# A windowed-attention backward kernel: stores moved to SyncE's queue a step later, gradient loads held behind a transpose

## The chip, the cores and the metric

The kernel runs on one core of one Trainium2 chip. The core has five engines with their own instruction queues: TensorE (PE in the profile, with PEld for its weight loads), VectorE (DVE), ScalarE (ACT), GpSimd (POOL) and SyncE (SP, which only issues transfers and waits). Transfers between device memory and on-chip memory are carried by 16 DMA engines; SP and ACT issue onto hardware queues (q1 is SP's, q10 is ACT's), GpSimd onto a software queue (q0). An instruction queue is in order: while an instruction waits for a semaphore or is being issued, everything behind it on that engine waits too.

The metric is device time in microseconds (us) of one execution, lower is better. Before the change three executions took 1948.42, 1941.60 and 1948.11 us, median 1948.11.

## The reference, cut to what matters

`x` and `grad_out` are 256 x 256 x 384 images in bf16. Both are cut into 1024 windows of 8 x 8 tokens. Each window does single-head attention over its 64 tokens with 384 channels, and the outputs are the forward result and the gradients for `x`, `wqkv` and `wo`:

```python
xw  = windows of x                      # (1024, 64, 384)
qkv = xw @ wqkv;  q, k, v = split(qkv)
p   = softmax(q @ k.T * C ** -0.5)      # (1024, 64, 64)
out = (p @ v) @ wo, windows put back    # out_0
out_1, out_2, out_3 = vjp(out)(grad_out)  # d x, d wqkv, d wo
```

## The kernel before, in words

**Tiling.** Windows are taken eight at a time, as a *quad*: four tiles of 128 partitions, each holding two windows of 64 tokens. There are 128 quads. `load` (L122) brings a quad's `x` into `xq` with four DMAs of 96 KB on SP's queue and its `grad_out` into `dq` with four on GpSimd's queue. One such DMA covers 16 image rows of 8 tokens of 384 channels, that is 128 rows of 768 bytes. `xq` has ten buffers, `dq` six.

**Algebra.** The projections are folded into 384 x 384 weight products (`A_sb`, `AT_sb`, `B_sb`, `BT_sb`) at the start. Per quad the kernel needs `x` and `grad_out` with channels on the partitions (`xT`, `dT`), which `load_turn` (L129) makes with two DMA transposes on SP's queue; for the first quads (`G_ON_PE`, `X_ON_PE`) TensorE does it. `dT` has two buffers, `xT` three.

**Stages.** The work is software-pipelined over quads in `step(c, b, a, ahead)` (L334), called for i = -1 to 128 with a = quad i+1, b = quad i, c = quad i-1, ahead = quad i+3:

- `scores`, `soft` and `uv` of quad i (b); at the end of the softmax `turn` (L237) transposes `ps` into `PS` by a DMA transpose on SP.
- `project(0)` of quad i+1 (a), which reads `dT`; later `project(1)`, which reads `xT`; `gather` on VectorE packs both into `zy`, and `to_tokens` (L169) transposes `zy` into `tok` by the largest DMA transpose, on SP.
- `load(ahead)`: the eight loads of quad i+3.
- `attend` of quad i-1 (c), in two halves, tiles (0, 1) and (2, 3): all products that need `PS` and `tok`. Its results leave PSUM by ScalarE and VectorE copies into `o` and `d` buffers of the pool `ob`, which has eight of each; a quad uses four of each. Each half then issues its stores on GpSimd's queue (L298 to L305): four in the first half, five in the second, seven of them 96 KB and two of 48 KB.
- `filler` (L326) runs pieces of the weight gradients (`gf_group`) between.

**Order.** The schedule is manual: each engine executes its instructions in the order in which the program emits them. So SP's order in every step of the middle is `PS` of quad i, four `x` loads of quad i+3, `tok` of quad i+1, then (from `load_turn` at the top of the next step) `dT` and `xT` of quad i+3: eight DMAs per step. GpSimd's order is four `dq` loads, four stores, five stores. Every DMA of a queue is given one of eight completion semaphores in rotation and waits until the DMA that had it before has landed.

Of the kernel before, what the change touches and what calls it, by code (L numbers as in the profile page):

```python
# [11 lines left out]
BF16 = mybir.dt.bfloat16  # L12
# [10 lines left out]
def kernel(  # L23
# [21 lines left out]
    nc = tc.nc  # L45
# [9 lines left out]
    sm = ctx.enter_context(tc.tile_pool(name="sm", bufs=2))  # L55
# [18 lines left out]
    def fetch_weights():  # L74
        nc.sync.dma_start(out=w_sb[:, :, columns(2)], in_=w_in[:, :, columns(2)])
        nc.scalar.dma_start(out=wo_sb[:], in_=wo.rearrange("(m p) n -> p m n", p=P))
        for k in (0, 1):
            nc.scalar.dma_start(out=w_sb[:, :, columns(k)], in_=w_in[:, :, columns(k)])
# [32 lines left out]
    def weight_rest():  # L111
        weight_product(B_sb, wT[2], wo_sb, None)
        weight_product(AT_sb, wT[1], wT[0], scale)

    def windows(ap, st, first, count=2):
        row, col = st["at"]
        return ap[0, row + WIN * first:row + WIN * (first + count), col:col + WIN, :]

    LO, HI = slice(0, WT), slice(WT, P)
    OTHER = {0: HI, WT: LO}  # L120

    def load(st):  # L122
        st["xq"] = xq = grp.tile([P, QUAD, C], BF16, tag="xq", name="xq", bufs=2 * GQ + 4)
        st["dq"] = dq = qp.tile([P, QUAD, C], BF16, tag="dq", name="dq", bufs=6)
        for t in range(QUAD):
            nc.sync.dma_start(out=xq[:, t, :], in_=windows(x, st, 2 * t))
            nc.gpsimd.dma_start(out=dq[:, t, :], in_=windows(grad_out, st, 2 * t))  # L127
# [55 lines left out]
    def over_k(ap, n=P):  # L183
        return ap.unsqueeze(2).broadcast_to([n, QUAD, WT])

    def soft(st, step):
        sd = st["sd"]
        if step == 0:
# [53 lines left out]
    def operand(st, n, t, h):  # L242
        if n in ("PT", "ST"):
            return st["PS"][h, t, int((n == "ST") == (h == LO)), :]
        if n in ("z", "y"):
            return st["tok"][h, int(n == "y"), :, t, :]
        return st[n][h, t, :]

    def attend(st, pair):
        if pair[0] == 0:  # L250
            st["Uq"] = grp.tile([P, QUAD, C], BF16, tag="Uq", name="Uq")
            st["Wq"] = grp.tile([P, QUAD, C], BF16, tag="Wq", name="Wq")

        def bank(name):
            return ring.tile([P, C], F32, tag="r", name=name)

        def slot(straight, crossed, start=False, stop=False):
            for h in (LO, HI):
                dst, lhs, rhs, t = straight
                products = [(h, dst[h, :], lhs, rhs, t, {"start": True, "stop": True})]  # L260
                lhs, rhs, t = crossed
                o = OTHER[h.start]
                dst = pd[int((t == t0) == (h == LO))]
                products.append((o, dst[o, :], lhs, rhs, t, {"start": start, "stop": stop}))
                for o, dst, lhs, rhs, t, flags in products if h == LO else products[::-1]:
                    nc.tensor.matmul(dst, lhsT=operand(st, lhs, t, h), rhs=operand(st, rhs, t, h), **flags)  # L266

        def keep(name, src):
            sb = ob.tile([P, C], BF16, tag=name, name=name)
            nc.scalar.copy(out=sb[:], in_=src[:])  # L270
            return sb

        t0, t1 = pair
        pw = {t: bank("pw") for t in pair}
        pu = {t0: bank("pu")}
        pd = [bank("pd") for outer in (0, 1)]
        po = {t0: bank("po")}
        pu[t1] = bank("pu")
        po[t1] = bank("po")
        slot((pw[t0], "Pb", "dq", t0), ("Pb", "z", t0), start=True)  # L280
        nc.scalar.copy(out=st["Wq"][:, t0, :], in_=pw[t0][:])  # L281
        slot((pw[t1], "Pb", "dq", t1), ("dS", "y", t0))
        nc.vector.tensor_copy(out=st["Wq"][:, t1, :], in_=pw[t1][:])
        slot((pu[t0], "ST", "xq", t0), ("Pb", "z", t1), start=True)
        nc.vector.tensor_copy(out=st["Uq"][:, t0, :], in_=pu[t0][:])
        slot((po[t0], "PT", "uq", t0), ("dS", "y", t1))
        o0 = keep("o", po[t0])
        slot((pu[t1], "ST", "xq", t1), ("ST", "vq", t0), stop=True)
        nc.vector.tensor_copy(out=st["Uq"][:, t1, :], in_=pu[t1][:])
        slot((po[t1], "PT", "uq", t1), ("ST", "vq", t1), stop=True)  # L290
        o1 = keep("o", po[t1])
        inner = keep("d", pd[0])
        if t0 == 0:
            st["mid"], st["rim"] = [ob.tile([P, C], BF16, tag="d", name="d") for k in range(2)]
        upper, lower = (st["rim"], st["mid"]) if t0 == 0 else (st["mid"], st["rim"])
        nc.scalar.copy(out=lower[LO, :], in_=pd[1][LO, :])
        (nc.scalar.copy if t0 else nc.vector.tensor_copy)(out=upper[HI, :], in_=pd[1][HI, :])
        nc.gpsimd.dma_start(out=windows(out_0, st, 2 * t0), in_=o0[:])  # L298
        nc.gpsimd.dma_start(out=windows(out_0, st, 2 * t1), in_=o1[:])
        nc.gpsimd.dma_start(out=windows(out_1, st, 2 * t0 + 1), in_=inner[:])  # L300
        if t0 == 0:
            nc.gpsimd.dma_start(out=windows(out_1, st, 0, 1), in_=st["rim"][HI, :])
        else:
            nc.gpsimd.dma_start(out=windows(out_1, st, 3), in_=st["mid"][:])
            nc.gpsimd.dma_start(out=windows(out_1, st, 7, 1), in_=st["rim"][LO, :])  # L305

    fill = []

# [17 lines left out]
    def filler(n):  # L326
        while n and fill:
            try:
                next(fill[0])
                n -= 1  # L330
            except StopIteration:
                fill.pop(0)

    def step(c, b, a, ahead):  # L334


        def on(st):
            return (lambda f, *r: f(st, *r)) if st is not None else (lambda f, *r: None)
        C_, B, A = on(c), on(b), on(a)
        B(scores)  # L340
        B(soft, 0)
        if b is not None and c is None:
            weight_rest()
        B(uv, 0, 0)
        B(uv, 0, 1)
        B(soft, 1)
        B(uv, 1, 0)
        B(uv, 1, 1)
        B(soft, 2)
        B(soft, 3)  # L350
        B(uv, 2, 0)
        B(uv, 2, 1)
        B(uv, 3, 0)
        B(uv, 3, 1)
        B(soft, 4)
        for mo in range(CK):
            A(project, 0, mo)
        B(soft, 5)
        B(turn)
        if ahead is not None:  # L360
            load(ahead)
        filler(1)
        C_(attend, (0, 1))
        A(gather, 0)
        for mo in range(CK):
            A(project, 1, mo)
        A(gather, 1)
        A(to_tokens)
        filler(1)
        C_(attend, (2, 3))  # L370

    G_ON_PE, X_ON_PE = 4, 1
    EV = {"z": "AAA", "y": "AAA", "u": "AAAA", "v": "AAAA", "o": "AAAA", "U": "DDDD", "W": "DDDD", "d": "AAAA"}
    quads = [(row, col) for row in range(0, H, 2 * WIN * QUAD) for col in range(0, W, WIN)]
    sts = [{"at": q, "i": i} for i, q in enumerate(quads)]
    n = len(sts)
    AHEAD = 3
# [40 lines left out]
    with tc.manual_schedule(engines=MANUAL):  # L418
        fetch_weights()
        warm_up(9)  # L420
        load(sts[0])
        make_identity(nc, ident[:])
        load(sts[1])
        load(sts[2])
        load_turn(sts[0])
        load_turn(sts[1])
        turn_blocks(wT[2], w_sb, 2 * CK)
        weight_product(BT_sb, wo_sb, wT[2], None)
        turn_on_pe(sts[0], "dq", "dT")
        turn_on_pe(sts[0], "xq", "xT")  # L430
        turn_blocks(wT[0], w_sb, 0)
        turn_blocks(wT[1], w_sb, CK)
        weight_product(A_sb, wT[0], wT[1], scale)
        nc.vector.memset(GF_acc[:], 0.0)
        held = []
        last = None
        get = lambda i: sts[i] if 0 <= i < n else None
        for i in range(-1, n + 1):
            if 0 <= i < n - 2:
                load_turn(sts[i + 2])  # L440
            step(get(i - 1), get(i), get(i + 1), get(i + AHEAD) if i >= 0 else None)
            if 0 < i + 2 < G_ON_PE:
                turn_on_pe(sts[i + 2], "dq", "dT")
            if i == 1:
                turn_blocks(woT_sb, wo_sb)
            if i > 0:
                held.append(sts[i - 1])
                sts[i - 1] = None
            if held and i == n:
                last = gf_group(held, True)  # L450
            elif len(held) == GQ:
                fill.append(gf_group(held))
                held = []
        filler(1 << 30)
        weight_gradients(last)
# [30 lines left out]
```

## Time and profile before

| what | value | where it is read |
|---|---|---|
| three executions | 1948.42, 1941.60, 1948.11 us | the times |
| span of the profiled execution | 1942.8 us | head of the page |
| its own total beside the span | not given apart; its span lies between the lowest and the median time | |
| DVE busy | 1458.9 us (75%) | part 1 of the page |
| ACT busy | 1546.3 us (80%) | part 1 |
| POOL busy | 895.2 us (46%) | part 1 |
| data moved | 423.21 MB, mean 218 GB/s | part 3 |
| granted TensorE clock | 0.999 on average | the view of cores |

The page counts computing instructions and GpSimd's DMA instructions as busy time, but not SP's: for SP, which only issues DMAs, one has to read its instruction queue (the timeline or a line's own view, where SPq stands for it). A DMA has two durations: that of the instruction on the queue that issues it, and the time from issue to landing. In a line's view, three numbers with slashes are the minimum, median and maximum duration in ns.

### The profile page before, as it was taken

Reading aid. Unit: us, or ns where it says so; the run is one execution under the profiler, and the core shown is the slowest. Engines: PE = TensorE matmul, PEld = TensorE weight load, DVE = VectorE, ACT = ScalarE, POOL = GpSimd, SP = SyncE. Lnnn points to the kernel's source line nnn. Section 1 sums busy time; section 2 is a strip of 40 time slices with the busy share of each in tenths; the row PEclk is TensorE's granted clock in tenths of the full one; section 3 lists DMA queues with packets and bytes.
Section 4 is the critical chain, followed back from the end, with each engine's and each line's share of the span. In section 5 each row is a group of like instructions: output and inputs, shape, how many; then the busy total and the mean of one; then the engine's idle time right before and its main releaser. Section 6 shows DMA issues by size and latency. Waiting matters only on the chain.

```text
span 1942.8 us, 48771 instructions
## 1 busy us (share of the span) xinstructions
PE 1926.6 (99%) x17859; PEld 1076.9 (55%) x17859; DVE 1458.9 (75%) x3244; ACT 1546.3 (80%) x3613; POOL 895.2 (46%) x1670
## 2 busy tenths in 40 slices
PE   9999999999999999999999999999999999999999
PEld 5555555555555555555555555555555555555555
DVE  6777767777777777777777777777777777777776
ACT  7878878778777878887787878788887878887775
POOL 3445444444444445444444454454444445444432
PEclk9999999999999999999999999999999999999999
DMA  8999999999999999999999999999999999999994
GB/s 186 220 222 227 224 204 222 224 217 224 223 221 226 226 220 223 226 221 220 219 228 222 221 219 229 221 225 217 230 218 228 224 219 220 226 224 219 222 195 109
DMA packets 1017584, 423.21 MB, mean 218 GB/s; under 512 B 899584, under 2 KB 992768, under 8 KB 1017344
## 3 DMA queue, kind: packets, MB, share of 16 engines
q1 hardware_dynamic: 935984, 267.85, 79.0%
q0 software_dynamic: 79872, 151.17, 30.8%
q8 instruction: 140, 2.29, 0.5%
q10 hardware_dynamic: 1488, 1.08, 0.2%
q14 instruction: 100, 0.82, 0.1%
HBM read 101.84 MB, written 101.84 MB: 105 GB/s over the span
## 4 chain that ended last, share of the span: by engine, by line
PE 94%; ACT 2%; DMA 2%; DVE 1%; issue 0%; SPq 0%; POOL 0%; ACTq 0%; POOLq 0%
PE pj L145 49%; PE pg L145 25%; PE pw L266 6%; PE sd L145 5%; PE pu L266 4%; PE po L266 4%; DMA PS<-ps 1%; DMA dT<-dq 1%; PE pd L266 1%; ACT uq L235 0%; ACT vq L235 0%; DMA dq<-in_grad_out_dram 0%; ACT yz L159 0%; PE pe L385 0%; SPq L134 0%
## 5 line engine op out<-in xcount | busy, mean ns | idle before, releaser
L298 POOL DMA_DIRECT2D out_dram<-o x256 | 137.7, 538 | 936.8 <-ACT o L270 915.8
L145 PEld LDWEIGHTS <-xq 128*128 128x128 bf16 x3072 | 300.0, 98 | 226.4 <-issue 2.0
L145 PEld LDWEIGHTS <-xT 128*128 128x128 bf16 x3072 | 291.6, 98 | 182.7
L145 PE MATMUL pj<-B_sb,xT 128*128 128x384 bf16 x1536 | 333.5, 326 | 0.0
L145 PE MATMUL pj<-AT_sb,xT 128*128 128x384 bf16 x1536 | 333.3, 326 | 0.0
L127 POOL DMA_DIRECT2D dq<-in_grad_out_dram x512 | 271.9, 547 | 40.4 <-DMA out_dram<-o 17.6
L281 ACT CAST Wq<-pw 128x384 bf16<-128x384 f32 x256 | 123.0, 480 | 200.1 <-PE pw L266 200.0
L145 PE MATMUL pj<-dT,BT_sb 128*128 128x512 bf16 x1152 | 271.3, 381 | 5.1 <-DMA dT<-dq 5.1
L145 PE MATMUL pg<-Uq,xq 128*128 128x384 bf16 x1536 | 270.4, 326 | 0.5 <-DVE GF_acc L321 0.5
L145 PE MATMUL pj<-xT,A_sb 128*128 128x512 bf16 x1152 | 270.8, 380 | 0.0
L145 PE MATMUL pg<-Wq,xq 128*128 128x384 bf16 x1536 | 270.4, 326 | 0.0
L321 DVE TENSOR_TENSOR GF_acc<-pg,GF_acc 128x384 f32<-128x384 f32 x258 | 143.9, 558 | 152.8 <-PE pg L145 152.7
L235 ACT CAST uq<-pj 128x384 bf16<-128x384 f32 x512 | 249.9, 488 | 7.3 <-PE pj L145 1.0
L235 ACT CAST vq<-pj 128x384 bf16<-128x384 f32 x512 | 255.1, 498 | 0.1
L270 ACT CAST o<-po 128x384 bf16<-128x384 f32 x512 | 220.9, 484 | 5.1 <-PE po L266 2.4
L211 ACT COPY ps<-Pb 64x256 bf16<-64x256 bf16 x256 | 103.2, 403 | 149.7 <-DVE Pb L208 148.2
L159 ACT CAST yz<-pj 128x512 bf16<-128x512 f32 x384 | 206.7, 644 | 2.1 <-PE pj L145 2.0
L161 ACT CAST yz<-pj 128x512 bf16<-128x512 f32 x384 | 200.8, 607 | 0.2
L145 PEld LDWEIGHTS <-BT_sb 128*128 128x128 bf16 x1152 | 112.4, 98 | 129.8 <-DMA dT<-dq 7.0
L145 PEld LDWEIGHTS <-A_sb 128*128 128x128 bf16 x1152 | 102.3, 98 | 139.9 <-issue 33.6
L167 DVE COPY zy<-yz 128x1536 bf16<-128x1536 bf16 x256 | 143.4, 560 | 46.3 <-ACT yz L161 39.8
L266 PE MATMUL pd<-tok,Pb 64*64 64x384 bf16 x1024 | 173.3, 335 | 0.0
(89 smaller groups left out, 3376.1 us busy)
## 6 DMA issues: line engine op xcount, KB each, us to landing
xq<-in_x_dram SPq DMA_DIRECT2D x512, 96.0 KB, 4.2
dq<-in_grad_out_dram POOLq DMA_DIRECT2D x512, 96.0 KB, 4.0
out_dram<-o POOLq DMA_DIRECT2D x512, 96.0 KB, 4.0
out_dram<-d POOLq DMA_DIRECT2D x384, 96.0 KB, 4.2
out_dram<-d POOLq DMA_DIRECT2D x256, 48.0 KB, 4.3
tok<-zy SPq DMA_TRANSPOSE x128, 7.6
PS<-ps SPq DMA_TRANSPOSE x128, 4.7
xT<-xq SPq DMA_TRANSPOSE x127, 6.3
```

The costliest lines, as they stand in the source:

```text
L127: nc.gpsimd.dma_start(out=dq[:, t, :], in_=windows(grad_out, st, 2 * t))
L145: nc.tensor.matmul(out, lhsT=lhsT, rhs=rhs, start=start, stop=stop)
L159: ENG[EV["z"][mo]](out=yz[:, mo, :, 0:4:3, :], in_=pj[:])
L161: ENG[EV["y"][mo]](out=yz[:, mo, :, 1:3, :], in_=pj[:])
L167: nc.vector.tensor_copy(out=st["zy"][:, kind, :, :, :, :], in_=src)
L211: nc.scalar.copy(out=ps[h, :, w, :], in_=Pb[h, :, :])
L235: cp(out=dst[:, t, :], in_=pj[:])
L266: nc.tensor.matmul(dst, lhsT=operand(st, lhs, t, h), rhs=operand(st, rhs, t, h), **flags)
L270: nc.scalar.copy(out=sb[:], in_=src[:])
L281: nc.scalar.copy(out=st["Wq"][:, t0, :], in_=pw[t0][:])
L298: nc.gpsimd.dma_start(out=windows(out_0, st, 2 * t0), in_=o0[:])
L321: nc.vector.tensor_tensor(out=GF_acc[:, f, ma, :], in0=pw[:], in1=GF_acc[:, f, ma, :], op=ALU.add)
```

## The change

Two things are changed. First, `attend` no longer issues its stores: it notes them in `st["kept"]`, and a new function `store` issues them. In the step of index i the stores of quad i-2 (argument `d`) go out on SP's queue right behind the `x` loads; only the last quad's stores still go to GpSimd, in the step that computes them. Second, before GpSimd issues the `dq` loads of quad i+3, it copies two elements of the `dT` tile of quad i+2 into a small tile `seen`; that copy waits for the DMA transpose of quad i+2 to land, so the loads behind it are held until then.

SP's order in a step becomes: `PS`, four `x` loads, nine stores, `tok`, `dT`, `xT`, 17 DMAs in place of 8. GpSimd's becomes: copy into `seen`, four `dq` loads. The orders on TensorE, VectorE and ScalarE are as before.

```diff
-    def load(st):
+    def load(st, behind=None):
         st["xq"] = xq = grp.tile([P, QUAD, C], BF16, tag="xq", name="xq", bufs=2 * GQ + 4)
         st["dq"] = dq = qp.tile([P, QUAD, C], BF16, tag="dq", name="dq", bufs=6)
+        if behind is not None:
+            seen = sm.tile([1, 2], BF16, tag="seen", name="seen")
+            nc.gpsimd.tensor_copy(out=seen[:], in_=behind["dT"][0:1, 0, 0, 0:2])
         for t in range(QUAD):
             nc.sync.dma_start(out=xq[:, t, :], in_=windows(x, st, 2 * t))
             nc.gpsimd.dma_start(out=dq[:, t, :], in_=windows(grad_out, st, 2 * t))
...
-        nc.gpsimd.dma_start(out=windows(out_0, st, 2 * t0), in_=o0[:])
-        nc.gpsimd.dma_start(out=windows(out_0, st, 2 * t1), in_=o1[:])
-        nc.gpsimd.dma_start(out=windows(out_1, st, 2 * t0 + 1), in_=inner[:])
+        kept = [(out_0, 2 * t0, 2, o0[:]), (out_0, 2 * t1, 2, o1[:]), (out_1, 2 * t0 + 1, 2, inner[:])]
         if t0 == 0:
-            nc.gpsimd.dma_start(out=windows(out_1, st, 0, 1), in_=st["rim"][HI, :])
+            kept.append((out_1, 0, 1, st["rim"][HI, :]))
         else:
-            nc.gpsimd.dma_start(out=windows(out_1, st, 3), in_=st["mid"][:])
-            nc.gpsimd.dma_start(out=windows(out_1, st, 7, 1), in_=st["rim"][LO, :])
+            kept += [(out_1, 3, 2, st["mid"][:]), (out_1, 7, 1, st["rim"][LO, :])]
+        st.setdefault("kept", []).extend(kept)
+
+    def store(st, queue):
+        for ap, first, count, sb in st.pop("kept", ()):
+            queue.dma_start(out=windows(ap, st, first, count), in_=sb)
...
-    def step(c, b, a, ahead):
+    def step(d, c, b, a, ahead, behind):
...
         if ahead is not None:
-            load(ahead)
+            load(ahead, behind)
+        if d is not None:
+            store(d, nc.sync)
         filler(1)
         C_(attend, (0, 1))
+        if c is not None and c["i"] == n - 1:
+            store(c, nc.gpsimd)
...
         C_(attend, (2, 3))
+        if c is not None and c["i"] == n - 1:
+            store(c, nc.gpsimd)
...
-            step(get(i - 1), get(i), get(i + 1), get(i + AHEAD) if i >= 0 else None)
+            step(get(i - 2), get(i - 1), get(i), get(i + 1), get(i + AHEAD) if i >= 0 else None,
+                 get(i + 2) if i + 2 >= G_ON_PE else None)
...
-                sts[i - 1] = None
+            if i > 1:
+                sts[i - 2] = None
```

## The prediction

> **What bounds the kernel now.** I read first the page's busy times, the DMA queues and the chain that ended last.
>
> ```profile
> span 1942.8 us, 48771 instructions
> PE 1926.6 (99%) x17859; PEld 1076.9 (55%) x17859; DVE 1458.9 (75%) x3244; ACT 1546.3 (80%) x3613; POOL 895.2 (46%) x1670
> q1 hardware_dynamic: 935984, 267.85, 79.0%
> q0 software_dynamic: 79872, 151.17, 30.8%
> PE 94%; ACT 2%; DMA 2%; DVE 1%; issue 0%; SPq 0%; POOL 0%; ACTq 0%; POOLq 0%
> ```
>
> TensorE is the bound: busy 99%, 94% of the chain. All its idle time is 1942.8 - 1926.6 = 16.2 us. By stages, 6.7 us of that lie between 100 and 1900 us, the rest in the start and the tail. Once, around 280 us, it also cost clock: a stretch of 15 us has a granted clock of 0.89, so 15 x 0.11 = 1.7 us. About 8 us are thus all that an edit of the middle can win, 0.4%.
>
> The chain in order of time gives the step: the same group of 33 matmuls begins every 14.79 us.
>
> ```profile
> 788.24 5.84 PE pj L145 x33
> 803.03 5.84 PE pj L145 x33
> ```
>
> The change touches SP's queue, which the page does not count, so I read SP's timeline over one step (777.68 to 792.47, again 14.79 us).
>
> ```profile
> 777.68 5.15 SPq L171 DMA_TRANSPOSE tok<-zy  x1
> 783.06 1.46 SPq L134 DMA_TRANSPOSE dT<-dq  x1
> 784.70 2.76 SPq L134 DMA_TRANSPOSE xT<-xq  x1
> 787.62 1.68 SPq L239 DMA_TRANSPOSE PS<-ps  x1
> 789.35 3.02 SPq L126 DMA_DIRECT2D xq<-in_x_dram  x4
> 792.47 4.77 SPq L171 DMA_TRANSPOSE tok<-zy  x1
> ```
>
> This is the finding: SP is full. Its eight DMAs take 5.15 + 1.46 + 2.76 + 1.68 + 3.02 = 14.07 us of 14.79 just to issue, and no gap exceeds 0.25 us. It holds no real wait: `tok` goes out at 792.47 although its input is packed long before. In the timeline of a step 177 us earlier VectorE packs it at 608.2 and SP issues `tok` at 615.8; `PS`, whose input is ready at 602.8, leaves at 610.8. SP runs some 8 us late and keeps pace with TensorE with nothing to spare.
>
> Then what each DMA costs its queue, from the lines' own views (minimum/median/maximum in ns):
>
> ```profile
> L171 SPq DMA_TRANSPOSE tok<-zy x128: 3607/4768/6755, 18.9 to 1900.3; - x128
> L134 SPq DMA_TRANSPOSE xT<-xq x127: 1432/2944/5716, 12.9 to 1887.1; - x127
> L134 SPq DMA_TRANSPOSE dT<-dq x124: 1422/1578/3497, 49.2 to 1884.3; - x124
> L239 SPq DMA_TRANSPOSE PS<-ps x128: 1188/1426/2388, 28.9 to 1909.9; - x128
> L126 SPq DMA_DIRECT2D xq<-in_x_dram x512: 536/600/1881, 1.2 to 1879.5; - x171
> L416 SPq DMA_DIRECT2D out_dram<-dw x1: 344/344/344, 1939.8 to 1939.8; - x1
> ```
>
> An `x` load has a firm price (median 600, minimum 536). The transposes stretch, up to twice their minimum: they are held up by traffic, and this part can shrink.
>
> **The change part by part.**
>
> *Stores onto SP.* Nine per step, for quads 0 to 126: 127 x 9 = 1143 more issues on a queue that has 1024 in the whole loop now. No SP store of this shape is in the trace. Low end: the 96 KB `dw` store on SP, 0.34 us. High end: the `x` load, 0.60 us, with the same 16-row window, size and queue. I take 0.55, near the `x` load, because it has the same mismatch of 16 image rows against 128 partitions. On GpSimd's queue, loads and stores of this window differ little (547 against 538 ns). On SP, the 3 x 128-row weight load took 0.45 and the store 0.37, which scales 0.60 to 0.50. Between instructions SP loses 0.04 us (four loads in 2.52 us at 0.60 each, at 30.09 us). The two half-size stores count full: on GpSimd one took 573 against 533. So 9 x 0.59 = +5.3 us per step; ends 9 x 0.38 = 3.5 and 9 x 0.64 = 5.8.
>
> *Transposes with less beside them.* In the step shown, SP's five groups exceed their minima by 1.54 + 0.04 + 1.33 + 0.49 + 0.50 = 3.9 us (the four loads against 2.52). At best all of it goes; at worst nothing, since the same bytes still cross the same 16 DMA engines. Stores are two thirds of q0's bytes (per quad 768 of 1152 KB), which gives 2.6. The held `dq` loads then fall beside `x` loads and stores, whose issue doesn't stretch, so the saving should be nearer the top: I take 3.2.
>
> *Sum for SP.* 14.8 + 5.3 - 3.2 = 16.9 us per step, against 14.8 that TensorE needs; ends 14.8 + 3.5 - 3.9 = 14.4 and 14.8 + 5.8 = 20.6. SP becomes the bound, and TensorE waits 2.1 us per step. 127 x 2.1 = 267 us; the 8 us of hiccups drown in it. 1942.8 + 267 - 8 = 2202, say 2200 us. The profiled span is 5.3 us below the median of the three runs (1948.1); I let that lie in the range.
>
> *Stores off GpSimd.* Removed: nine issues of about 0.54 us, 4.9 us per step, off the path now (POOL idles 915.8 us for ScalarE's `o` copies), so worth nothing by themselves. A DMA page of the Trainium skill ("DMA: Bandwidth & Descriptors", section "Rules for kernel authors") says that spreading DMAs over issuing engines brings no bandwidth and only saves sequencer issue time. It speaks against this change: by it, gathering the stores on one queue loses 9 issues and wins no transfer time, so 14.8 + 5.3 = 20.1 us per step and about 2600 us. The same page's section "Issuing engine by pattern" calls the hardware path generally faster and puts simple stores on Sync; the rows do not bear that out for issuing (`x` load on SP 600 ns, `dq` load on GpSimd 547).
>
> *A step's delay of the stores.* `o` and `d` have eight buffers, four per quad, so quad i's copies wait for quad i-2's stores. Those stores now stand behind `PS` and four loads, and the ninth lands about 1.7 + 3.0 + 5.3 + 4.2 (landing of an `x` load) = 14 us after `PS` is issued. In the step shown that is 787.6 + 14 = 802, whereas ScalarE copies `d` at 797.6. So SP has to run some 4 us earlier than now. It can while it has slack (its `PS` data are 8 us old). Without slack this is where TensorE will be stopped: ScalarE late on the stores, `yz` and PSUM behind it. This sets where the stall appears; its size is SP's sum above.
>
> *The eight semaphores.* A DMA waits for the one eight before it. Eight stores take 8 x 0.59 = 4.7 us and an `x` load lands in 4.2 (median, maximum 7.3): 0 us mostly, at most 2.6 in a step; taken as 0.
>
> *The hold on GpSimd.* The two-element copy costs between 0.10 us (a GpSimd memset) and 0.29 (its select), on an otherwise empty queue. Behind it stand only four loads; who waits for them is `dT` of quad i+3 on SP, and everything behind that. From `dT` issue to the next: landing 6.1 + copy 0.3 + four issues 2.2 + landing 4.0 = 12.6 us, under a step of 14.8 and more so of 16.9. Cost 0. If a transpose lands at its longest, 11.7 us, the sum is 18.2 and SP loses 1 to 3 us in that step.
>
> **Rivals.**
>
> *SP still fits (not slower).* If stores cost like the `dw` store (0.38 with the gap) and the transposes fall to their minima, SP needs 14.4 us and TensorE stays the bound. The point from which this decides is 9 x (price + 0.04) = saving: a price of 0.39 us at the full saving of 3.9, 0.25 at 2.6. For it: transposes that stretch to twice their minimum. Against: 512 `x` loads at a median of 0.60. It gives 1942.8 - 8 = 1935 us without the hiccups, up to 1948 with them.
>
> *The DMA engines set the pace.* q1's packets fill 79.0% of the span; with two thirds of q0's 30.8% they fill 99.5%. If both queues' shares, 110.6%, had to run one after the other, a step would take 1.106 x 14.8 = 16.4 us: 1942.8 + 127 x 1.6 - 8 = 2138 us. For it: the stretched transposes. Against: q1 shares time with q0 now, and its packets should shorten. The sign would be stores far over 0.6 us each.
>
> *The hold binds.* SP's issue fits, but `dT` is late for its `dq` loads. The margin is 14.8 - 12.6 = 2.2 us, so it decides from landings 2.2 us above their medians. At 0.1 to 0.5 us per step: 1955 to 2006 us. Against: the issue sum.
>
> **How the numbers follow.** SP's issue sum as the bound: 0.70. With 0.50 per store and the saving of 3.9 a step is 15.8 us, 2060 us; with 0.60 and 2.6 it is 18.0, 2340. DMA engines: 0.08. Hold: 0.06. SP fits: 0.16, of it 0.09 within 0.5% and 0.07 faster by more than 0.5% (below 1938.4; about 0.5% is what a measurement here can tell from no change). Slower is thus 0.84. The range leaves out most of the not-slower case below and the dearer half of the unknowns above: 1955 to 2340. Within the likeliest case alone it is 2060 to 2340.
>
> **What would show it.** Right: SP's timeline again without gaps, nine `out_dram` rows of 0.5 to 0.6 us each per step, `tok` about 3.8 and `xT` about 2 us, steps near 16.9 us; TensorE's busy share down to about 88%, its waits and ScalarE's led by transfers (`out_dram`, `PS`, `dT`); GpSimd nearly idle. Wrong: store rows near 0.35 us with SP waiting for semaphores at `PS` or `tok` and a step of 14.8 (SP fits); store rows of 1 us and more (DMA engines); SP idle ahead of `dT` until `dq` lands (hold). If the transposes keep their medians, the time goes toward 2340 and beyond.

## The result and the profile after

The changed kernel takes 2346.70 us in the median of four executions (2343.00 to 2350.43). The kernel before, run beside it, took 1946.96 us in the median of four. The ratio is 1.206, with a 95% interval of 1.2036 to 1.2083: about 400 us slower, where 2200 us was forecast with a range of 1955 to 2340. The direction and the place were right, the size was not. The profiled execution took 2344.89 us with a span of 2343.1. Every median here and below is over the executions of a kernel that lie within 1.5% of its fastest; only `e3_hold_only` has others, two of six.

From the page of the changed kernel come the span, the busy time of the engines, the two DMA queues and the chain that ended last:

```profile
span 2343.1 us, 47493 instructions
PE 2091.0 (89%) x17859; PEld 1118.9 (48%) x17859; DVE 1458.3 (62%) x3244; ACT 1574.7 (67%) x3613; POOL 297.5 (13%) x650
q1 hardware_dynamic: 1082288, 367.79, 77.1%
q0 software_dynamic: 25008, 51.15, 8.1%
SPq 37%; PE 19%; ACT 18%; DMA 13%; DVE 8%; issue 5%; POOL 0%; ACTq 0%; DVEq 0%; POOLq 0%
```

TensorE is no longer the bound (89%), and the largest share of the chain that ended last is SPq, SyncE's instruction queue (37%). GpSimd went from 46% to 13%. The DMA engines are not fuller than before: q1's share of the span fell from 79.0% to 77.1% although it carries 100 MB more.

SP's timeline of one step of the changed kernel (start, duration, line, what):

```profile
897.23 3.62 SPq L174 DMA_TRANSPOSE tok<-zy  x1
901.08 1.45 SPq L137 DMA_TRANSPOSE dT<-dq  x1
902.58 1.81 SPq L137 DMA_TRANSPOSE xT<-xq  x1
904.55 1.46 SPq L242 DMA_TRANSPOSE PS<-ps  x1
906.07 2.58 SPq L129 DMA_DIRECT2D xq<-in_x_dram  x4
908.69 1.24 SPq L310 DMA_DIRECT2D out_dram<-o  x2
909.97 1.27 SPq L310 DMA_DIRECT2D out_dram<-d  x2
911.29 1.66 SPq L310 DMA_DIRECT2D out_dram<-o  x2
913.00 1.91 SPq L310 DMA_DIRECT2D out_dram<-d  x3
915.02 3.64 SPq L174 DMA_TRANSPOSE tok<-zy  x1
```

From `tok` to `tok` are 17.8 us, and again no gap exceeds 0.25 us: SP is full and now longer than TensorE's 14.8 us. The four groups of stores take 1.24 + 1.27 + 1.66 + 1.91 = 6.1 us. The rest takes 3.62 + 1.45 + 1.81 + 1.46 + 2.58 = 10.9 us, where the same five groups took 14.1 before. In this step the stores cost 6.1 and gave 3.2 back.

The views of those lines give the prices (minimum/median/maximum in ns):

```profile
L310 SPq DMA_DIRECT2D out_dram<-d x635: 537/604/1987, 59.0 to 2320.9; - x159
L310 SPq DMA_DIRECT2D out_dram<-o x508: 542/597/1638, 57.7 to 2319.0; - x170
L137 SPq DMA_TRANSPOSE xT<-xq x127: 1441/1839/3938, 13.0 to 2283.4; - x127
L137 SPq DMA_TRANSPOSE dT<-dq x124: 1325/1432/2274, 48.0 to 2282.0; - x124
L174 SPq DMA_TRANSPOSE tok<-zy x128: 3568/3658/4837, 18.7 to 2304.6; - x128
```

A store costs what an `x` load costs (its median was 600). The transposes fell toward their minima: `tok` from a median of 4.77 to 3.66 us, `xT` from 2.94 to 1.84.

The table of waits (us in total, times, longest) shows where the other engines meet the late queue:

```profile
POOL seen L127 <- DMA dT<-dq: 1922.8, 123, 37.4
DVE d L300 <- DMA out_dram<-d: 268.5, 68, 5.9
ACT d L299 <- DMA out_dram<-d: 228.8, 121, 3.9
ACT o L273 <- DMA out_dram<-o: 122.2, 83, 3.2
```

ScalarE and VectorE wait for stores that have not landed, because their buffers can't be written before; TensorE then waits for them. GpSimd's 1922.8 us in the hold is an engine that has nothing else to do. TensorE's granted clock is lower too (0.963 on average, 0.999 before); with TensorE idle for 11% of the span, nothing here shows that this added to the time.

### The profile page after: what moved, and what is told of

It is laid out like the page before. It is cut to its first block, busy times and chain, and to the rows that moved or that the text cites. A ratio compares the mean times of both kernels' runs of the same rounds, so it can differ in the third digit from the quotient of the medians.

```text
span 2343.1 us, 47493 instructions
## 1 busy us (share of the span) xinstructions
PE 2091.0 (89%) x17859; PEld 1118.9 (48%) x17859; DVE 1458.3 (62%) x3244; ACT 1574.7 (67%) x3613; POOL 297.5 (13%) x650
## 3 DMA queue, kind: packets, MB, share of 16 engines
q1 hardware_dynamic: 1082288, 367.79, 77.1%
## 4 chain that ended last, share of the span: by engine, by line
SPq 37%; PE 19%; ACT 18%; DMA 13%; DVE 8%; issue 5%; POOL 0%; ACTq 0%; DVEq 0%; POOLq 0%
SPq L310 18%; SPq L129 12%; DMA out_dram<-d 12%; PE pj L148 9%; ACT yz L164 7%; PE sd L148 5%; SPq L242 4%; ACT uq L238 3%; ACT vq L238 3%; DVE GF_acc L326 3%; DVE zy L170 3%; SPq L137 3%; PE po L269 2%; PE pg L148 2%; ACT ex L203 2%
## 5 line engine op out<-in xcount | busy, mean ns | idle before, releaser
L148 PEld LDWEIGHTS <-xT 128*128 128x128 bf16 x3072 | 309.4, 104 | 213.3 <-issue 48.6
L273 ACT CAST o<-po 128x384 bf16<-128x384 f32 x512 | 237.1, 485 | 253.4 <-DMA out_dram<-o 122.2
L300 DVE CAST d<-pd 64x384 bf16<-64x384 f32 x128 | 71.8, 561 | 488.1 <-DMA out_dram<-d 268.5
L148 PE MATMUL pj<-B_sb,xT 128*128 128x384 bf16 x1536 | 363.3, 349 | 0.0
L148 PE MATMUL pj<-AT_sb,xT 128*128 128x384 bf16 x1536 | 354.4, 342 | 0.0
L148 PE MATMUL pj<-dT,BT_sb 128*128 128x512 bf16 x1152 | 270.0, 379 | 15.6 <-DMA dT<-dq 14.8
L299 ACT CAST d<-pd 64x384 bf16<-64x384 f32 x256 | 122.1, 477 | 228.8 <-DMA out_dram<-d 228.8
L127 POOL COPY seen<-dT 1x2 bf16<-1x2 bf16 x123 | 24.2, 197 | 1922.8 <-DMA dT<-dq 1922.8
L269 PE MATMUL po<-uq,PS 64*64 64x384 bf16 x1024 | 180.0, 334 | 96.7 <-DVE GF_acc L326 95.9
L269 PE MATMUL pw<-dq,Pb 64*64 64x384 bf16 x1024 | 153.7, 338 | 103.5 <-ACT yz L164 102.9
L269 PEld LDWEIGHTS <-PS 64*64 64x64 bf16 x3072 | 136.5, 105 | 196.2 <-issue 168.8
```

Of the source, the lines that this page charges most:

```text
L148: nc.tensor.matmul(out, lhsT=lhsT, rhs=rhs, start=start, stop=stop)
```

## The experiments

The table gives SP's step in each kernel, averaged over 100 steps of its trace (from `tok` number 11 to 111); "transposes" is the mean of `tok`, `dT`, `xT` and `PS` added, "direct" that of loads and stores. The rest of a step lies between the instructions, mostly 0.04 to 0.25 us each, or is a real wait.

| kernel | DMAs on SP per step | step, us | transposes | direct on SP | median time, us |
|---|---|---|---|---|---|
| before | 8 | 14.89 | 11.2 | 2.8 | 1946.96 |
| changed | 17 | 18.11 | 8.8 | 8.1 | 2346.70 |
| e1_no_hold | 17 | 19.56 | 10.2 | 8.2 | 2506.51 |
| e4_half_bytes | 17 | 18.08 | 8.8 | 8.1 | 2342.71 |
| e5_ten_buffers | 17 | 18.10 | 8.7 | 8.2 | 2334.40 |
| e13_flat_stores | 17 | 17.36 | 8.9 | 7.3 | 2240.04 |
| e7_x_on_pool | 13 | 16.04 | 9.3 | 5.5 | 2085.98 |
| e6_four_on_sp | 12 | 15.85 | 9.8 | 5.1 | 2055.11 |
| e12_six_only | 14 | 16.17 | 8.9 | 6.2 | 2100.50 |
| e11_four_only | 12 | 14.77 | 8.7 | 5.1 | 1934.46 |
| e9_no_stores | 8 | 14.80 | 8.4 | 2.6 | 1934.75 |
| e2_late_on_pool | 8 | 16.16 | 12.6 | 2.5 | 2122.27 |
| e3_hold_only | 8 | 16.83 | 13.4 | 2.5 | 2161.58 |
| e14_hold_behind_tok | 8 | 15.64 | 12.2 | 2.5 | 2031.58 |
| e10_late_on_pool_no_hold | 8 | 14.89 | 11.2 | 2.7 | 1938.91 |
| e8_before_x_on_pool | 4 | 15.06 | 13.8 | 0 | 1967.07 |

### Is it the number of issues, the bytes, or the buffers?

Half the bytes in the same stores:

```diff
-            queue.dma_start(out=windows(ap, st, first, count), in_=sb)
+            queue.dma_start(out=windows(ap, st, first, count)[:, :, 0:C // 2], in_=sb[:, 0:C // 2])
```

> The changed kernel with the same 1143 stores on SP, each of half its bytes (only the first 192 of 384 channels of out_0 and out_1 are written, for all quads). Theory (the number of issues on SP sets the pace): within 1.5% of 2346.7, store rows still near 0.60 us. Rival (the DMA engines' transfer time sets the pace): a step loses about half of the stores' transfer time of some 2.3 us, so 127 x 1.1 = 140 us less, near 2205.

2342.71 us, ratio 1.2084 (1.2054 to 1.2115), against 1.206 of the changed kernel: halving the stores' bytes changes nothing, and the stores' medians stay at 0.60 us. The DMA engines had less to do: q1's packets fill 70.7% of the span in place of 77.1%. Their number is the same, though, so e4 tests the bytes alone. For the packets there is e11 below, which issues four stores per quad: q1 fills more of its span, at a time of 1934 us. So the DMA engines are not the pace. The rows of q1, first e4, then e11:

```profile
q1 hardware_dynamic: 1082288, 317.85, 70.7%
q1 hardware_dynamic: 999992, 311.57, 82.3%
```

More buffers for what is stored:

```diff
-    ob = ctx.enter_context(tc.tile_pool(name="ob", bufs=8))
+    ob = ctx.enter_context(tc.tile_pool(name="ob", bufs=10))
...
-        st["dq"] = dq = qp.tile([P, QUAD, C], BF16, tag="dq", name="dq", bufs=6)
+        st["dq"] = dq = qp.tile([P, QUAD, C], BF16, tag="dq", name="dq", bufs=5)
```

> The changed kernel with ten o and ten d buffers in place of eight (and five dq buffers in place of six, to make room). In the changed kernel ScalarE and VectorE wait longest for out_dram, that is for buffers whose stores have not landed. Theory (SP's issue rate sets the pace, the buffer wait is only where it shows): within 1% of 2346.7. Rival (too few buffers is the cause): half a step of 18 us more of slack takes those waits away, below 2200.

2334.40 us, ratio 1.1991 (1.1973 to 1.2009), half a per cent less. The three waits for `out_dram` in the table of waits above are gone from the top of its own table (268.5 us became 24.1), and others stand in their place:

```profile
DVE GF_acc L326 <- PE pg L148: 482.7, 211, 7.0
ACT Wq L284 <- PE pw L269: 401.8, 246, 2.7
PEld L148 <- DMA dT<-dq: 326.2, 121, 4.3
PE pj L148 <- DMA dT<-dq: 268.8, 113, 4.0
```

TensorE now waits for `dT`, another transfer of the same late queue. The waits for buffers were where the delay surfaced, not its cause.

Fewer stores, the rest left out:

```diff
         if d is not None:
+            d["kept"] = d["kept"][0:4]    # e12: [0:6]; e9: d.pop("kept") and no store
             store(d, nc.sync)
```

> The changed kernel that leaves out the stores of quads 0 to 126 altogether (out_0 and out_1 are not written, except for the last quad). Theory: SP's eight DMAs are back inside the step with room, 11.4 us of issuing in 14.8, so TensorE sets the pace and the time is 1930 to 1945; SP now shows real waits, tok near 3.7 us and xT near 1.9. If the transposes' stretch came from something other than the stores (own backlog), tok stays near 4.8 and xT near 2.9 and SP stays full. Rival (the hold costs): clearly above 1960.

> The changed kernel that issues only the first four of each quad's nine stores (out_0 rows of tiles 0 and 1, out_1 rows of two pieces), on SP; the other five are left out, so out_0 and out_1 are written in part. Without any store SP had 3.0 us of real waits per step. Theory (SP's issuing is free as long as it fits into TensorE's 14.8 us): four stores need 4 x 0.67 = 2.7 us, they just fit, and the time stays at 1933 to 1950 us. Rival (each store on SP costs its share, 400 / 9 = 44 us): near 2110.

> The same with the first six of nine stores on SP, three left out. Theory: 6 x 0.67 = 4.0 us against 3.0 of room, a step of 15.8 us, 1935 + 127 x 1.0 = 2065 us (2030 to 2100). Rival (share per store): 1935 + 6 x 44 = 2200.

With none 1934.75 us, with four 1934.46, with six 2100.50, with nine 2346.70. Four stores are free, as the sum of 4 x 0.67 = 2.7 us against some 3 us of room said; in e11 SP is just full, with 1.0 us of a step outside its instructions against 3.8 in e9. From six to nine the price is (2346.70 - 2100.50) / 3 = 82 us per store, which over 127 steps is 0.65 us. Going back from six by two such prices, one arrives at 1936 us: the bend lies at four stores. Six came out 35 us above the estimate, 0.5 us beyond its bounds: the estimate had kept the transposes at e9's 8.4 us per step, and with six stores they took 8.9. In e9 SP has real waits, here before `xT`, `PS` and `tok`:

```profile
898.67 3.65 SPq L174 DMA_TRANSPOSE tok<-zy  x1
902.55 1.44 SPq L137 DMA_TRANSPOSE dT<-dq  x1
904.50 1.42 SPq L137 DMA_TRANSPOSE xT<-xq  x1
908.23 1.19 SPq L242 DMA_TRANSPOSE PS<-ps  x1
909.48 2.97 SPq L129 DMA_DIRECT2D xq<-in_x_dram  x4
913.47 3.64 SPq L174 DMA_TRANSPOSE tok<-zy  x1
```

From 905.92 to 908.23 SP waits for `PS`, from 912.45 to 913.47 for `tok`. This is what a queue with room looks like; the timeline of before has no such place.

### What moving DMAs between the queues does

Four of nine stores on SP, and, in another kernel, the `x` loads off SP:

```diff
-        for ap, first, count, sb in st.pop("kept", ()):
-            queue.dma_start(out=windows(ap, st, first, count), in_=sb)
+        for k, (ap, first, count, sb) in enumerate(st.pop("kept", ())):
+            (queue if k < 4 else nc.gpsimd).dma_start(out=windows(ap, st, first, count), in_=sb)
```

```diff
-            nc.sync.dma_start(out=xq[:, t, :], in_=windows(x, st, 2 * t))
+            nc.gpsimd.dma_start(out=xq[:, t, :], in_=windows(x, st, 2 * t))
```

> The changed kernel with four of the nine stores on SP and the other five on GpSimd, all still a step late. Theory (each store costs SP 0.63 + 0.04 us and spares the transposes 2.8/9 = 0.31 us): a step of 14.8 + 4 x 0.67 - 4 x 0.31 = 16.2 us, 1943 + 127 x 1.4 - 8 = 2115 us, between 2060 and 2170. Rival (a fixed price of having any store on SP, or of storing a step late): stays near 2340. Rival (buffers freed too late by the ninth store alone): near 1950 to 2000.

> The changed kernel with the four x loads moved from SP to GpSimd: 13 DMAs on SP in place of 17, nine of them stores, the same transfers in all. Theory (SP's issue sum): a step of 18.1 - 2.5 - 0.2 = 15.4 us, up to 15.8 if the x loads now stretch the transposes; 1943 + 127 x (0.6 to 1.0) - 8 = 2010 to 2062 us. Rival (the stores as such, by their kind or by the buffers that they hold, cost the time): stays above 2250.

2055.11 and 2085.98 us. Both go the way of the issue sum, neither hits it: the first lies 5 us below its range, the second 24 us above. In e7 the loads' 2.5 us went, but the transposes grew from 8.8 to 9.3. Now the same `x` loads are moved in the kernel before:

> The kernel before with its four x loads on GpSimd in place of SP: SP has the four transposes only. Theory (SP was full before, and this caused the few waits of TensorE): SP's busy sum falls to 9 to 11.5 us with real waits, a step of 14.80 us throughout, 1931 to 1940 us. If the waits had another cause (single slow transfers), it stays with before within 0.3%. GpSimd's 17 issues take 17 x 0.54 = 9.2 us of a step; if they come to bind, above 1960.

This missed. It is 1.3% slower than before (1967.07 us, ratio 1.013, 1.0095 to 1.0165). SP has only four DMAs per step, and yet it is nearly full:

```profile
894.70 6.84 SPq L171 DMA_TRANSPOSE tok<-zy  x1
901.75 2.95 SPq L134 DMA_TRANSPOSE dT<-dq  x1
904.88 3.38 SPq L134 DMA_TRANSPOSE xT<-xq  x1
908.41 1.62 SPq L239 DMA_TRANSPOSE PS<-ps  x1
910.13 7.04 SPq L171 DMA_TRANSPOSE tok<-zy  x1
```

`tok` takes 6.8 to 7.0 us to issue, against 3.65 in e9. Taking 2.8 us of issues off SP added 2.5 us to its transposes (13.75 against 11.2 per step, in a traced execution of 1983.54 us). What runs beside them did change: while one `tok` was being issued, packets of the software queue kept the 16 DMA engines busy for 1.3 us in the mean before and for 3.1 us in e8 (their time during the issue, divided by 16).

### The hold

> The changed kernel without the hold: the copy into `seen` is not issued, the stores stay on SP a step late. Theory (SP's issuing sets the pace, 18.1 us per step): the hold is off the path, so within 1.5% of the changed kernel's 2346.7, rather above it than below (2340 to 2385), since the gradient loads may now fall beside the transposes and stretch them by up to 0.3 us per step. Rival (the hold makes `dT` late): the time falls clearly, below 2250.

The edit passes `None` for `behind`, so no copy into `seen` is issued. 2506.51 us, ratio 1.2928 (1.2882 to 1.2974): with the stores on SP the hold saves 160 us. The sign was expected, the size lies far above the bound given. Two lines of SP's timeline and one of GpSimd's show how: the four gradient loads, no longer held, are issued right ahead of `dT`, so that they are under way during `dT` and `xT`, and these take 2.15 and 3.12 us in place of 1.45 and 1.81. In the mean, the loads' packets kept the DMA engines busy for 0.6 us of a `dT` and 1.0 of an `xT`; in the changed kernel none fell there.

```profile
912.39 2.15 SPq L137 DMA_TRANSPOSE dT<-dq  x1
914.59 3.12 SPq L137 DMA_TRANSPOSE xT<-xq  x1
```

```profile
910.43 2.09 POOL L130 DMA_DIRECT2D dq<-in_grad_out_dram  x4 [16.57 <-PE pu L269]
```

Then the stores were put back on GpSimd's queue, with and without the hold and the delay (e2: `store(d, nc.gpsimd)`, with the hold; e10: the same and `None` for `behind`; e3: `attend` calls `store(st, nc.gpsimd)` at its end, with the hold).

> The changed kernel with its stores on GpSimd's queue again: still a step late, still behind the hold, but SP has its eight DMAs of before. Theory (only the nine issues on SP cost; the delay and the hold do not): SP has room, because stores and gradient loads now go out after `dT` has landed and miss the transposes; tok near 3.8 us, a step of 14.80 us, 1932 to 1943 us, that is 0 to 0.6% faster than before. Rival (the step's delay or the hold costs by itself): above 1960.

> The kernel before with the hold alone: stores in their old place on GpSimd, as soon as they are computed, but now behind the held gradient loads. Theory: the second half's stores still fall beside tok and dT, so SP keeps part of its stretch (a busy sum between 12 and 14 us of 14.8) and TensorE stays the bound: 1933 to 1950 us, within 0.5% of before. Rival (the hold delays the stores behind it until buffers run out): above 1960.

> The stores a step late on GpSimd, without the hold: the fourth corner beside the changed kernel (SP, hold), the one without hold (SP, no hold) and the one on GpSimd with hold (2122 us). Theory (SP's transposes are stretched by whatever the software queue sends while they are being issued, and the hold fixes the burst of 13 transfers onto tok): without the hold the burst goes out as one piece early in the step, beside x loads and tok; tok between 4.8 and 6.3 us, a step of 14.8 to 16.0 us, 1940 to 2090 us, below 2122. Rival (the step's delay itself costs): 2122 or more.

| median, us | hold | no hold |
|---|---|---|
| stores on SP, a step late | 2346.70 | 2506.51 |
| stores on GpSimd, emitted a step late | 2122.27 | 1938.91 |
| stores on GpSimd, old place | 2161.58 | 1946.96 (before) |

The first two expectations failed. The hold does cost by itself, 183 us (e2 against e10) and some 217 (e3 against the 1944.40 of before beside it), once GpSimd also carries the stores. And delaying the stores in program order does nothing on GpSimd's queue; the early burst that was expected of e10 did not come. In e10 GpSimd comes to the stores before their data are there and issues them as soon as ScalarE is done. Its wait for that is the wait of before (first e10, then before):

```profile
POOL out_dram L310 <- ACT o L273: 914.1, 251, 23.9
POOL out_dram L298 <- ACT o L270: 915.8, 251, 26.4
```

Its SP step is that of before to 0.01 us, and its ratio of 0.9967 (0.995 to 0.9984) lies within half a per cent. Against e10, e2's SP step is longer by 16.16 - 14.89 = 1.3 us, and the transposes alone grew by that much (12.6 against 11.2). Over 127 steps this is some 160 us, by which the two profiled spans differ (2101.4 and 1941.2).

In e2 GpSimd's queue shows one burst, and SP's shows what stands beside it:

```profile
917.74 0.18 POOL L127 COPY seen<-dT 1x2 bf16<-1x2 bf16 x1 [7.07 <-DMA dT<-dq]
918.30 2.12 POOL L130 DMA_DIRECT2D dq<-in_grad_out_dram  x4 [0.39 <-PE pg L148]
920.38 1.09 POOL L310 DMA_DIRECT2D out_dram<-o  x2
921.46 1.10 POOL L310 DMA_DIRECT2D out_dram<-d  x2
922.54 1.05 POOL L310 DMA_DIRECT2D out_dram<-o  x2
924.30 1.62 POOL L310 DMA_DIRECT2D out_dram<-d  x3 [0.70 <-DMA dq<-in_grad_out_dram]
```

```profile
917.25 1.49 SPq L242 DMA_TRANSPOSE PS<-ps  x1
918.79 2.50 SPq L129 DMA_DIRECT2D xq<-in_x_dram  x4
921.40 7.37 SPq L174 DMA_TRANSPOSE tok<-zy  x1
```

The landing of `dT` releases all 13 transfers at once, from 918.3 to 925.9, and seven of the nine stores fall on `tok`, which takes 7.37 us to issue. To test that the place of this burst matters, it was released by another landing, that of quad i's `tok` (`behind` is then quad i in place of i+2):

```diff
-            nc.gpsimd.tensor_copy(out=seen[:], in_=behind["dT"][0:1, 0, 0, 0:2])
+            nc.gpsimd.tensor_copy(out=seen[:], in_=behind["tok"][0:1, 0, 0, 0, 0:2])
```

> Stores a step late on GpSimd with a hold as in e2_late_on_pool (2122 us), but held behind the landing of tok of quad i in place of dT of quad i+2, which lands one DMA later on SP. Theory (what counts is where the burst of 13 transfers falls): it now starts some 2 to 5 us earlier, beside dT, xT, PS and the x loads, and is over when the next tok is issued; tok falls from a median of 6.4 us to 3.7 to 4.5, dT and xT grow to 2 to 3.5 each, SP's step is 14.8 us or little more, 1933 to 1990 us. Rival (a hold on GpSimd's queue costs by its waiting): stays at 2080 to 2170.

2031.58 us, ratio 1.0445 (1.0413 to 1.0477): between the two. Moving the release took half of the hold's cost away, so a hold as such has no fixed price. But the gain did not come where it was expected: `tok` stayed at a median of 6.36 us (6.44 in e2), and the burst still reached into it. Of the 0.5 us by which SP's step is shorter than in e2, `dT` gave 0.25 and `xT` 0.14. The hold's cost thus lies in the stretched transposes; that it comes from the burst's overlap with them, and from nothing else, is argued, not shown.

### What sets the price of a store on SP

```diff
-            queue.dma_start(out=windows(ap, st, first, count), in_=sb)
+            flat = ap.rearrange("b h w c -> (b h w) c")
+            at = st["i"] * QUAD * P + first * WT
+            queue.dma_start(out=flat[at:at + count * WT, :], in_=sb)
```

> The changed kernel with the same nine stores on SP, the same tiles and bytes, but each written to 128 (or 64) consecutive rows of out_0 and out_1 in place of its 16 x 8 window, so the rows of the outputs are in the wrong order. If the window's shape sets the price on SP, a store costs about 0.35 us like the dw store of the trace before, a step is 18.1 - 9 x 0.27 = 15.7 us, and the time is 1943 + 127 x 0.9 - 8 = 2050 us (2000 to 2100). If the price is that of any 96 KB transfer on a busy SP queue, store rows stay at 0.60 us and the time within 1.5% of 2346.7.

2240.04 us, between the two forecasts. The view of its store lines:

```profile
L312 SPq DMA_DIRECT2D out_dram<-d x635: 332/467/2363, 60.7 to 2224.3; - x159
L312 SPq DMA_DIRECT2D out_dram<-o x508: 332/578/2107, 59.6 to 2222.9; - x170
```

The minimum falls to 0.33 us, near the 0.34 of the `dw` store before, from 0.54: the window's shape accounts for 0.2 us of the cheapest store. In the mean of 100 steps a store fell only from 0.63 to 0.53 us. What else holds a store up to 0.47 or 0.58 us when it goes out behind others stays open.

## Why the prediction was off, point by point

- *SP is the queue that counts, and it is full.* Right. The signs named for it came: no gaps on SP, TensorE's busy share near 88% (89), `tok` about 3.8 us (3.66), `xT` about 2 (1.84), ScalarE's waits led by `out_dram`, GpSimd nearly idle. The step near 16.9 us did not come; it took 18.1. e4, e5 and e11 exclude bytes, buffers and the mere presence of stores on SP, and e9 shows that without the stores the loss is gone.
- *The price of a store, 0.55 us: the term that failed.* It measured 0.63 in the mean over 100 steps (nine take 5.64 us), 0.60 in the median, so even the high end of 0.60 was too low. The discount for stores came from two weight transfers at the ends of the kernel; the row nearest in shape and queue, the `x` load, had the right price, and its mean of 0.70 us (four take 2.78 per step) would have warned that the median is a low end. 5.64 - 9 x 0.55 = 0.69 us per step, or 127 x 0.69 = 88 us.
- *The saving in the transposes, 3.2 us: too large, but inside the 2.6 to 3.9 that the range went by.* In the mean it is 2.7 (14.0 us of issuing before against 11.3 for the same instructions). It was read as an excess over minima in one step; the mean of many steps keeps some. 127 x 0.5 = 64 us.
- *The sum.* With both measured and 0.3 us more between the instructions, 14.9 + 5.6 + 0.3 - 2.7 = 18.1 us, the measured step. 2202 + 88 + 64 = 2354 us, within 8 us of the measured 2346.70, so these two terms account for the miss. The upper end of the range had paired 0.60 with a saving of 2.6 and stopped 7 us short: it had no room for a mean above the median.
- *The delay of the stores.* Right on where the stall appears; e5 shows that it is only that.
- *The hold, taken as 0.* As a wait it cost nothing here, but through what it keeps away from `dT` and `xT` it is worth 160 us. The prediction counted on it within its saving (held loads fall beside transfers that don't stretch) and did not price it apart.
- *The eight semaphores.* No sign of them: hardly a gap over 0.1 us stands before a store in SP's timeline (together below 0.04 us per step).
- *The rivals.* That SP still fits holds for up to four stores (e11), not for nine. That the DMA engines set the pace is excluded by e4 and e11, that the hold binds by e1. In the prediction's sum for the DMA engines, 110.6% is the sum of all five queues; q1 and q0 alone give 109.8%, and the same sum then ends near 2119 us in place of 2138.
- *The rule from the Trainium skill* ("DMA: Bandwidth & Descriptors", section "Rules for kernel authors": spreading DMAs over issuing engines only saves issue time). It pointed the right way; the estimate by it, 2600 us, is 253 us too high, where the forecast was 147 too low. The runs add what it leaves out: the queue on which a transfer stands also decides what it stretches, by 2.7 us per step here and by 2.5 in e8.

## What to carry to other kernels

A queue that only issues transfers can be the second bound of a kernel without appearing in any busy time: lay out one step of its timeline and see whether it ever waits. If it doesn't, a DMA added to it costs its full issue time, priced by the nearest row's mean and not its median, less what its leaving the other queue gives back. Up to the point at which the queue fills the cost is nothing (four stores free, then 82 us each). And before DMAs are moved to another queue, ask what is being issued there and beside it at that moment: here 2.8 us of issues taken off SP came back as 2.5 us of stretched transposes.

## What the runs showed of the hardware that was not expected

- The issue time of a DMA transpose is not a property of the transpose: `tok` took 3.66 us to issue in the median in the changed kernel, 4.77 before, 6.44 in e2 and 6.30 in e8. It is the same instruction in all four. What differs is the software queue: during one `tok` its packets kept the DMA engines busy for 0.0, 1.3, 2.0 and 3.1 us in the mean. Within e2 and e8, too, the longer issues are those with more of it (correlations of 0.82 and 0.78). Why it stretches a transpose's issue, no run here shows.
- A queue can be full at just the pace of another bound. Before, SP's step was 14.89 us with 0.05 us of real waits in it, and TensorE's 14.8; with the stores left out SP's own need was 11.9 (14.8 less some 2.9 of waits). SP's backlog did not grow: it issued `tok` 7 us after its input was packed in the median of 100 steps, early and late ones alike. Either the stretch shrinks as SP falls behind, or TensorE was held to SP's pace: 14.89 against e9's 14.80 is 11 us over 127 steps, and the two spans differ by 10.4. Neither was tested by itself.
- The same hold of the same loads had opposite signs: -160 us with the stores on SP, +183 with the stores on GpSimd. In e2 the wait held everything behind it on GpSimd's queue, and let 13 transfers go at once.
- No kernel here beats the one before clearly. With stores left out the floor is 1934.5 us, 0.6% below before, and the best complete variant (e10) took 1938.91, a ratio of 0.9967.
